# A first expert's weight chunks prefetched in every attention step, and its layer 1 begun one step later

## The chip, the cores and the metric

The kernel runs on one core of a Trainium2 chip. The metric is the device time of one execution in microseconds, the median of several runs.

## What is computed

Windowed attention with a few sink positions, then a mixture of experts on its output. A token goes to the best of four groups and to the best of four experts in it.

```python
B, H, S, D = 4, 8, 768, 64          # n_sink = 4, window = 128
keep = is_sink | in_window          # causal window of 128 positions
a = softmax(where(keep, q @ k.T / sqrt(D), -1e9))
x = (a @ v).transpose(0, 2, 1, 3).reshape(3072, 512)

g_logits = x @ w_group              # 512 x 4
e_logits = xg @ w_expert[g]         # 512 x 4 per group
h  = np.maximum(xg[mask_e] @ w1[g, e], 0.0)    # 512 x 1024
ye = h @ w2[g, e]                               # 1024 x 512
out[tok_idx] = combined[:, None] * ye           # both softmax weights
```

## The kernel before, in words

**Attention.** The 3072 tokens are 24 tiles of 128. The main loop runs over steps i = 0 to 25 and is a software pipeline: step i makes the scores of tile i, transposes the probabilities of tile i - 1 and copies them out of PSUM (`trans`, `evac`), multiplies tile i - 2 with its values in two blocks (`values(b, 0)` for the tile itself, `values(b, 1)` for the tile before and the sinks) and copies the result out (`out_evac`, the tile `xT`), and for tile i - 3 makes router logits and transposes back (`logits`, `natural`) and normalises and stores (`norm`, the tile `xt`). Steps 24 and 25 have no scores (they are not `live`). The values of tile 23 come in step 25, its logits behind the loop. All tiles share one PSUM bank `po` for the values and one pair of banks `tp` for the transposes.

**Routing.** Tokens are routed in four batches of six tiles. A generator emits the small VectorE operations of a batch in units; each step may take so many (`UNITS`, and 16 in steps 24 and 25). When the second batch has been counted, the largest expert so far is picked as first expert (`id0`); this happens in step 17. The first two gathers of its tokens are issued in steps 21 and 22, a third one ("late", from the third batch) behind attention.

**Weights.** A weight matrix of an expert comes in four chunks of 128x1024 floats (512 KB each): chunks 0 to 3 are the first expert's layer 1, 4 to 7 its layer 2, from 8 on comes the second expert. `prefetch` asks for chunks on SyncE's queue, into five raw buffers `rw` used in turn. `wjob` converts one: ScalarE copies it, rounded, to `whi`, and VectorE subtracts, `wlo = rw - whi`. In attention, step i's `wjob` casts the first half, the next step casts the second half, and the subtraction follows in the middle of the step behind that. From step 24 on a chunk is cast whole and subtracted at once.

**Layer 1 of the first expert** begins inside attention. `early_work` is a generator, `ew`: its first two turns transpose the two gathered token tiles, each further turn is one f of layer 1 (one of eight 128-column parts of the hidden layer, 12 matmuls of 128x256 over the four chunks; `ph` is its PSUM tile, `un` holds tokens and hidden values). Each engine executes its instructions in the order in which the program text emits them. An f is emitted at once, so a chunk that is not ready stops TensorE there. Behind attention `finish(ew)` runs the remaining f, then layer 2 of these tokens; on the way the late gather's tile is transposed (`xpose`). A small planner (`spend`) decides how many routing units and conversions are emitted behind each piece.

```python
if i > CHOOK and (i % 2 == 0 or i > NI - 4):
    prefetch(min(RAW, len(raws) + (1 if live else RAW)))
```

Of the kernel before, what the change touches and what calls it, by code (L numbers as in the profile page):

```python
# [24 lines left out]
NI = B * NT  # L25
# [3 lines left out]
NDC = DM // P  # L29
# [65 lines left out]
SNAP = 1  # L95
SNAPB = 2
DEPTH = 2
CHOOK = 15
PW = G + NE
WARM = 18  # L100
FILL = [8, 10, 6]
# [40 lines left out]
def moe_attention(tc, kqT, vN, vS, nsw, wgx, w1, w2, out):  # L142
    nc = Pinned(tc)
    v = nc.vector
    with ExitStack() as top, ExitStack() as att:
# [39 lines left out]
        def pair():  # L185
            return ps_p.tile([P, 2, 4 * P], F32, name="tp")

        def warm(k, dst=None):
            dst = pair()[:, 0, 0:192] if k and dst is None else dst
            for _ in range(k):  # L190
                nc.tensor.matmul(dst, wz[:, 0:P], wz, start=True, stop=True)
# [17 lines left out]
        def load_q(i):  # L209
            b, t = divmod(i, NT)  # L210
            nc.sync.dma_start(qb[:, i % NQ], kqT[b, t, :, KB:].rearrange("d (h q) -> d h q", h=HP))
# [138 lines left out]
        def put_gates(n):  # L350
            for _ in range(min(n, len(gates))):
                t, g = gates.pop(0)
                nc.sync.dma_start(xd[t * P:(t + 1) * P, DM:XW], g)
# [296 lines left out]
        def gather(r, j):  # L650
            w = min(P, CAPT[r] - j * P)
            cc = BASE[r] + j
            if (r, j) in TWIN:
                return
            for a, b in TWIN.items():
                if b[0:2] == (r, j):
                    wait_for(f"x{a[0]}")
                    w += 32
            xg[r, j] = t = gp.tile([P, XW], F32, name="xg")
            src = xd[0:sum(BATCHES[:(SNAP if j < EC else SNAPB) + 1]) * P] if r == 0 else xd  # L660
            nc.gpsimd.indirect_dma_start(
                out=t[0:w], out_offset=None, in_=src,
                in_offset=bass.IndirectOffsetOnAxis(ap=gidx[0:w, cc:cc + 1], axis=0))
# [6 lines left out]
        state = dict(issued=0, done=0, freed=0, credit=0.0, route=0.0, clk=0.0, at=0.0, dma=0.0, gap=PELAG, dve=0.0)  # L670

        def dve(us):
            state["dve"] = max(state["dve"], state["clk"]) + us
# [3 lines left out]
        def prefetch(depth):  # L677
            while len(raws) < depth and state["issued"] < len(chunks):
                k = state["issued"]
                if k - min([x[-1] for x in raws] + [x[-1] for x in held.values()], default=k) >= RAW + len(rawp) * RAWB:  # L680
                    return
                l, r, c = chunks[k]
                if (f"id{r}" if r < 2 else "eid") not in ready:
                    return
                state["issued"] += 1
                if r not in regs:
                    src = (eidi if r > 1 else eid01)[0:1, r:r + 1]
                    regs[r] = nc.nc.values_load(src, engines=[ENG.SP], min_val=0, max_val=NE - 1)
                e = bass.ds(regs[r], 1)
                rw = raw(k)[:, 0:F]  # L690
                if l == 1:
                    nc.sync.dma_start(rw, w1[e, c * P:(c + 1) * P, :].rearrange("o p f -> (o p) f"))
                else:
                    nc.sync.dma_start(rw.rearrange("p (k n) -> p k n", k=2),
                                      w2[e, 2 * c * P:(2 * c + 2) * P, :].rearrange("o (k p) n -> p (o k) n", p=P))
                state["dma"] = max(state["dma"], state["clk"] + DMALAG) + DMATIME
                if CAPT[r] <= 64:
                    held[l, r, c] = rw, k
                else:
                    raws.append((l, r, c, rw, state["dma"] + DMASLACK, k))  # L700

        def wjob(force=False):
            if tail:
                prefetch(RAW + RAWB)
            k = state["done"]
            if raws and not force and state["clk"] < raws[0][4]:
                return None
            if not raws or k >= state["freed"] + WBUF or (k % WBUF >= WA and len(wpool) < 2):
                return None
            l, r, c, rw, _, pos = raws.pop(0)  # L710
            wp = wpool[k % WBUF >= WA]
            hi = wp.tile([P, F], F32R, name="whi")
            lo = wp.tile([P, F], F32R, name="wlo")
            z = F if tail else F // 2
            nc.scalar.copy(hi[:, 0:z], rw[:, 0:z])

            def rest():
                v.tensor_tensor(lo, rw, hi.bitcast(F32), ALU.subtract)
                wt[l, r, c] = hi, lo
                if l == 2 and r in FEW:  # L720
                    held[l, r, c] = rw, pos
                if tail:
                    prefetch(RAW + RAWB)
            dve(1.2)
            state["done"] += 1
            if tail:
                rest()
                return True

            def more():  # L730
                nc.scalar.copy(hi[:, z:], rw[:, z:])
                return rest

            half.append(more)
            return None
# [442 lines left out]
        for i in range(NI + 2):  # L1178
            live = i < NI
            a, b, c = i - 1, i - 2, i - 3  # L1180
            mid, far, old = 0 <= a < NI, 0 <= b < NI, 0 <= c < NI
            state["clk"] += 3.0
            if i == NI:
                state.update(gap=0.0, dve=state["clk"])
                sps.close()
                put_gates(MAXB)
                while later:
                    gather(*later.pop(0))
                ps_h = fl.enter_context(tc.tile_pool(name="ps_h", bufs=4, space=PSUM, side="right", reuse_waits="tile"))
                tail.append(ps_h)  # L1190
                if rest:
                    rest()
                    rest = None
                if half:
                    half.pop()()()
            if live:
                scores(i, 0)
                scores(i, 1)
                if i + DEPTH < NI:
                    load_q(i + DEPTH)  # L1200
                warm(FILL[i] if i < len(FILL) else 0, ob[0][:, 224:416])
            if mid or old:
                env["tp"] = pair()
            if mid:
                trans(a)
                evac(a, 0)
                evac(a, 1)
            if far:
                values(b, 0)
                if b + 1 < NI:  # L1210
                    load_s(b + 1)
            if i + DEPTH < NI:
                load_k(i + DEPTH)
            if old:
                logits(c)
            if mid:
                sink_t(a)
            if old:
                natural(c)
            if live:  # L1220
                maxima(i, 0)
                exps(i, 0)
                maxima(i, 1)
            else:
                next(ew, None)
                if i == NI:
                    next(ew)
            if old:
                norm(c)
            routing(1, ("pe",))  # L1230
            if live:
                exps(i, 1, (0, 1))
            if mid:
                sink_evac(a)
            if live:
                exps(i, 1, (2, 3))
            if mid:
                sink_rows(a)
            if live:
                sink_pack(i)  # L1240
            if old:
                norm_logits(c)
            if i == 0:
                late_consts()
            state["clk"] += 3.0
            if far:
                values(b, 1)
                if live:
                    load_v(i)
                out_evac(b)  # L1250
            if rest:
                rest()
                rest = None
            put_gates(3 if live else MAXB)
            if live and later and not gates:
                gather(*later.pop(0))
            routing(UNITS.get(i, REND) if live else TSTEP, (None, "rd"))
            if live and i and i % 2 == 0:
                sums(i - 1)
            if i == NI:  # L1260
                sums(NI - 1)
            if live:
                rest = half.pop()() if half else wjob()
            if i > CHOOK and (i % 2 == 0 or i > NI - 4):
                prefetch(min(RAW, len(raws) + (1 if live else RAW)))
            if not live:
                wjob()
                next(ew, None)
        env["tp"] = pair()
# [308 lines left out]
```

## Time and profile before

| | before |
|---|---|
| median of 3 runs | 507.71 us (505.45 to 508.69) |
| profiled execution | 506.72 us, span 505.0 us |
| TensorE matmul, busy | 476.0 us, 94% of the span |
| VectorE / ScalarE / GpSimd busy | 376.5 / 329.6 / 168.9 us |
| TensorE's granted clock, mean | 0.979 |
| DMA traffic | 117.09 MB, mean 232 GB/s |

The span runs from the first to the last instruction. Granted clock is the share of full speed that TensorE's clock was given, 1.0 or 0.5 at a moment. Engines are PE (TensorE matmul), PEld (its weight load), DVE (VectorE), ACT (ScalarE), POOL (GpSimd), SPq (SyncE's DMA issues). In a timeline row the first number is the start in us, the second how long the instruction or the merged group took, then come engine, operation and out<-in tiles; a bracket gives the idle time of that engine just before, and what ended it. All kernel instructions go through one helper and so carry its line, 112.

### The profile page before, as it was taken

How to read it: one execution, taken by the hardware profiler on the slowest of the kernel's cores; microseconds unless marked ns; L12 is line 12 of the kernel's file. 1: busy time of each engine (PE TensorE's matmuls, PEld its weight loads, DVE VectorE, ACT ScalarE, POOL GpSimd, SP SyncE). 2: the span in 40 equal slices, each digit the busy share in tenths (PEclk: the TensorE clock that was granted, in tenths of full speed). 3: DMA queues.
4: the chain of work that ended last, by engine and by line, in shares of the span. 5: the costliest groups of instructions: out<-in, count | busy, mean ns of one | idle time of the engine just before them, and what ended most of it. 6: DMA issues, size and time to landing. Idle time of an engine off the chain costs nothing. (4 is left out here: it accounts for less than half of the span.)

```text
span 505.0 us, 14679 instructions
## 1 busy us (share of the span) xinstructions
PE 476.0 (94%) x5419; PEld 400.0 (79%) x5419; DVE 376.5 (75%) x1178; ACT 329.6 (65%) x856; POOL 168.9 (33%) x269
## 2 busy tenths in 40 slices
PE   7899999998975969999999999999999999999995
PEld 6688888877865958889798898759786878887974
DVE  7577898898866577997861775668767996999760
ACT  3999999888951234567742665557554786788651
POOL 3575765664680002403123120302330153102301
PEclk9999999999967999999999999999999999999998
DMA  8588888998893454684592446498669992999301
GB/s 237 166 270 271 286 265 252 266 300 231 279 312 105 159 198 142 201 295 163 203 411 86 121 145 228 123 353 324 201 245 334 387 380 88 326 369 380 122 0 49
DMA packets 59873, 117.09 MB, mean 232 GB/s; under 512 B 9758, under 2 KB 22046, under 8 KB 59792
## 3 DMA queue, kind: packets, MB, share of 16 engines
q1 hardware_dynamic: 54960, 102.50, 60.3%
q0 software_dynamic: 4304, 13.26, 8.1%
q8 instruction: 45, 0.74, 0.6%
q10 hardware_dynamic: 528, 0.29, 0.3%
q14 instruction: 36, 0.29, 0.2%
HBM read 103.25 MB, written 13.24 MB: 231 GB/s over the span
## 5 line engine op out<-in xcount | busy, mean ns | idle before, releaser
L112 DVE TENSOR_TENSOR wlo<-rw,whi 128x1024 fp32r<-128x1024 f32 x112 | 134.9, 1225 | 31.3 <-ACT whi L112 29.3
L112 PE MATMUL ph<-un,whi 128*128 128x256 f32 (+4 forms) x576 | 132.4, 318 | 1.2 <-ACT whi L112 1.0
L112 PE MATMUL po<-whi,un 128*128 128x512 f32 (+2 forms) x384 | 127.9, 396 | 0.0
L112 POOL DMA_INDIRECT out<-ot,sidx x33 | 42.8, 1298 | 239.0 <-ACT ot L112 96.3
L112 ACT CAST whi<-rw 128x1024 fp32r<-128x1024 f32 (+1 forms) x115 | 115.3, 1025 | 10.4 <-DMA rw<-in_w 6.7
L112 PE MATMUL ph<-un,wlo 128*128 128x160 f32 (+4 forms) x416 | 101.3, 268 | 4.4 <-DVE wlo L112 4.3
L112 PEld LDWEIGHTS ph<-un,whi 128*128 128x128 f32 x576 | 95.0, 191 | 3.2 <-ACT whi L112 1.2
L112 PEld LDWEIGHTS po<-whi,un 128*128 128x128 f32 (+1 forms) x384 | 70.8, 186 | 24.8 <-issue 6.7
L112 PEld LDWEIGHTS ph<-un,wlo 128*128 128x128 f32 x416 | 77.6, 190 | 5.7 <-DVE wlo L112 4.5
L112 ACT ACTIVATE pt<-sm,st 128x136 f32<-128x136 f32 x192 | 76.1, 402 | 6.6 <-DVE st L112 5.8
L112 PE MATMUL po<-wlo,un 128*128 128x512 f32 (+3 forms) x200 | 77.7, 390 | 2.2 <-DVE wlo L112 2.2
L112 DVE CUSTOM_DVE_ANT_0 sm<-ps,msk 128x136 f32<-128x136 f32 x192 | 45.8, 296 | 8.2 <-PE ps L112 1.7
L112 POOL DMA_INDIRECT xg<-xd,gidx x30 | 33.7, 1124 | 33.4 <-DMA rw<-in_w 21.0
L112 PEld LDWEIGHTS po<-wlo,un 128*128 128x128 f32 (+2 forms) x200 | 36.4, 182 | 10.1 <-DVE wlo L112 2.7
L112 PE MATMUL ps<-kb,qb 64*64 64x208 f32 (+1 forms) x768 | 39.2, 339 | 2.3 <-DMA qb<-in_kqT 1.8
L112 POOL COPY pu<-spT 32x512 f32<-32x512 f32 x48 | 29.8, 647 | 30.3 <-ACT spT L112 27.2
L112 ACT ACTIVATE un<-ph 128x256 fp32r<-128x256 f32 x40 | 15.3, 383 | 36.3 <-PE ph L112 35.5
L112 DVE TENSOR_TENSOR hc<-ph,hc 128x160 f32<-128x160 f32 (+2 forms) x64 | 21.8, 345 | 22.9 <-ACT hc L112 21.9
L112 ACT ACTIVATION_READ_ACCUMULATOR pt<-sm,st 128x1 f32 x192 | 36.8, 192 | 0.0
L112 ACT ACTIVATE ot<-po,cg 128x512 f32<-128x512 f32 (+3 forms) x25 | 17.0, 680 | 30.4 <-PE po L112 30.3
L112 PEld LDWEIGHTS ps<-kb,qb 64*64 64x64 f32 x768 | 27.1, 136 | 7.8 <-issue 3.4
L112 PE MATMUL po<-pa,vv 128*64 128x64 f32 x768 | 29.7, 233 | 3.4 <-POOL sp L112 1.8
(196 smaller groups left out, 726.1 us busy)
## 6 DMA issues: line engine op xcount, KB each, us to landing
rw<-in_w SPq DMA_DIRECT2D x128, 512.0 KB
vv<-in_vN SPq DMA_DIRECT2D x24, 512.0 KB
kb<-in_kqT SPq DMA_DIRECT2D x23, 288.0 KB
qb<-in_kqT SPq DMA_DIRECT2D x24, 256.0 KB
xd<-xt SPq DMA_DIRECT2D x24, 256.0 KB
vv<-in_vS SPq DMA_DIRECT2D x24, 128.0 KB
out<-ot,sidx POOLq DMA_INDIRECT x33, 8.3
xg<-xd,gidx POOLq DMA_INDIRECT x30, 5.4
```

The lines of the kernel that those rows point to most:

```text
L112: r = f(*a, **k)
```

## The change

Chunk prefetch starts at steps above 17 and is called in every step, not in every second one. At the start of step 24, conversions are forced until all four layer-1 chunks are done. At the ends of steps, `wjob` and a turn of `ew` come only behind step 24, so the first f of layer 1 moves from the end of step 24 to the middle of step 25 and the others follow one turn later.

```diff
-CHOOK = 15
+CHOOK = 17
...
                 if half:
                     half.pop()()()
+                while state["done"] < NDC:
+                    wjob(True)
             if live:
                 scores(i, 0)
...
-            if i > CHOOK and (i % 2 == 0 or i > NI - 4):
+            if i > CHOOK:
                 prefetch(min(RAW, len(raws) + (1 if live else RAW)))
-            if not live:
+            if i > NI:
                 wjob()
                 next(ew, None)
```

## Rows read from the trace of the kernel before

**Rows 1.** Windows by stage: PE, PEld, DVE, ACT, POOL busy us; clock, DMA share, GB/s.

```profile
130.00:140.00 10.00, 8.84 (x232) 7.48 (x224) 9.19 (x46) 9.48 (x34) 5.77 (x10) 1.00 0.97 310
...
150.00:160.00 10.00, 4.71 (x50) 3.90 (x48) 8.54 (x24) 2.96 (x5) 2.21 (x4) 0.84 0.42 139
```

**Rows 2.** Timeline of TensorE, from step 24 to the first expert's layer 2.

```profile
148.53 0.34 PE L112 MATMUL tp<-ident,sp 64*96 64x64 f32 x2 [0.55 <-POOL sp L112]
...
151.13 1.75 PE L112 MATMUL po<-pu,vv 96*64 96x64 f32 x32
...
159.94 0.58 PE L112 MATMUL ph<-un,wlo 128*128 128x256 f32 x1 [4.25 <-DVE wlo L112]
...
160.45 1.98 PE L112 MATMUL po<-pa,vv 128*64 128x64 f32 x32
...
166.45 1.15 PE L112 MATMUL po<-pu,vv 96*64 96x64 f32 x32
...
169.15 0.66 PE L112 MATMUL lg<-wsd,xT 128*64 128x40 f32 x16
...
169.74 0.47 PE L112 MATMUL tp<-ident,xT 64*128 64x64 f32 x8
...
173.69 0.46 PE L112 MATMUL ph<-un,whi 128*128 128x256 f32 x2
...
177.96 0.40 PE L112 MATMUL po<-whi,un 128*128 128x512 f32 x1
```

**Rows 3.** Timeline of VectorE and ScalarE in step 24.

```profile
151.00 0.69 DVE L112 TENSOR_TENSOR un<-ph,un 128x512 fp32r<-128x512 f32 x1 [3.26 <-ACT un L112]
...
153.59 0.59 ACT L112 COPY xT<-po 128x512 f32<-128x512 f32 x1
...
154.07 1.05 ACT L112 CAST whi<-rw 128x1024 fp32r<-128x1024 f32 x1
...
158.72 1.16 DVE L112 TENSOR_TENSOR wlo<-rw,whi 128x1024 fp32r<-128x1024 f32 x1
```

**Rows 4.** Timeline of ScalarE and VectorE at the start of step 24.

```profile
145.42 1.07 ACT L112 COPY pa<-tp 128x512 f32<-128x512 f32 x2
...
146.20 1.53 DVE L112 TENSOR_TENSOR wlo<-rw,whi 128x1024 fp32r<-128x1024 f32 x1
```

**Rows 5.** Timeline in step 21: a chunk's subtraction and GpSimd's select beside it.

```profile
128.70 1.22 DVE L112 TENSOR_TENSOR wlo<-rw,whi 128x1024 fp32r<-128x1024 f32 x1
128.77 1.66 POOL L112 TENSOR_SCALAR_AFFINE_SELECT pa<-pa 64x512 f32<-64x512 f32 x1
```

**Rows 6.** Timeline of GpSimd in step 24.

```profile
146.05 2.15 POOL L112 COPY pu<-spT 32x512 f32<-32x512 f32 x2
148.26 0.21 POOL L112 COPY sp<-pt 128x32 f32<-128x32 f32 x1
148.42 0.65 POOL L112 TENSOR_SCALAR_AFFINE_SELECT pu<-pa 64x512 f32<-64x512 f32 x1
```

**Rows 7.** Timeline of SyncE's DMA issues, steps 23 to 24.

```profile
143.91 4.23 SPq L112 DMA_DIRECT2D rw<-in_w  x4
```

**Rows 8.** Windows as in rows 1, finer, around the clock's changes.

```profile
152.00:153.00 1.00, 1.00 (x23) 0.93 (x20) 1.00 (x3) 0.00 (x0) 0.00 (x0) 0.75 0.78 250
...
158.00:160.00 2.00, 0.07 (x1) 0.07 (x1) 1.84 (x4) 0.00 (x0) 0.00 (x0) 0.83 0.18 16
...
166.00:167.00 1.00, 1.00 (x22) 0.87 (x22) 0.00 (x0) 0.38 (x1) 0.00 (x0) 0.93 0.16 57
```

**Rows 9.** Timeline behind attention: the late gather and two waits of TensorE.

```profile
175.75 0.97 POOL L112 DMA_INDIRECT xg<-xd,gidx  x1 [20.96 <-DMA rw<-in_w]
...
182.33 0.63 PE L112 MATMUL tp<-ident,xg 128*128 128x128 f32 x4 [1.61 <-DMA xg<-xd,gidx]
...
187.51 0.50 PE L112 MATMUL po<-wlo,un 128*128 128x512 f32 x1 [2.24 <-DVE wlo L112]
```

**Rows 10.** Waits of TensorE from 190 us: total, times, longest.

```profile
PE tp L112 <- DVE cg L112: 0.4, 1, 0.4
```

## Prediction

> **What bounds the kernel now.** I read the busy table by stage first, then TensorE's timeline where the table shows a hole, then what the other engines did at that moment, then the rest of the run. In attention all engines are near full and so is DMA, at 0.97 of its 16 engines [rows 1]. Between 150 and 160 us TensorE is busy for 4.71 of 10 us [rows 1]. Behind 190 us its longest kind of wait on a tile sums to 0.4 us [rows 10], so from there on TensorE sets the pace. What is won between 145 and 190 us therefore moves the end, if the weights and gathers move along.
>
> The hole is at the end of step 24 (the first step without scores). TensorE begins f=0 of the first expert's layer 1 and comes to weight chunk 3. It waits first for the high half and then 4.25 us for the low half [rows 2]. ACT cast the chunk at 154.07 us. DVE subtracts only at 158.72 us, because this subtraction stands behind the whole routing block of step 24 in DVE's program [rows 3]. Behind this wait, in TensorE's order, stands the rest of the last attention tile: its values start only at 160.45 us, its logits at 169.15 us [rows 2], though everything that the values need was ready some 6 us earlier (worked out below). A second price follows. The granted clock was 1.00 (2.4 GHz) before the wait. TensorE then idled for 4.25 us, the clock fell to half near 159.3 us (0.83 mean over 158 to 160) and rose again soon after 166 (0.93 over 166 to 167) [rows 8]. At half clock the 32 values matmuls took 1.98 us, at full clock 1.15 [rows 2].
>
> **The change, part by part.** I follow CHOOK, the prefetch condition, the forced conversion and the later layer 1.
>
> *Prefetch in every step.* Before, chunks 0 to 3 are asked for at the ends of steps 18, 20, 21 and 22, chunk 4 at the end of 23, chunks 5 to 7 at the start of 24. Afterwards steps 18 to 23 each ask for one (0 to 5), and the start of 24 asks for 6, 7 and 8. So on SP every old place carries the next chunk; step 19 gets a new load, and chunk 8 comes up from the end of step 24. CHOOK from 15 to 17 changes nothing: the expert's id is not known in step 16, and step 17 was odd. Conversion (half a chunk per step on ACT) keeps its slots: chunk 0 in 19 and 20, chunk 1 in 21 and 22, chunk 2 in 23 and 24. One more load of 512 KB enters the stretch before step 24. At the 310 GB/s of the nearest full stretch [rows 1] that is an estimated 1.7 us of DMA time. I cost it at nothing, since q, k and v are asked for up to two steps ahead; if that cover is gone, it costs 1.7 us. In step 24 SP waits for raw buffers: the four loads from 143.91 us take 4.23 us, the last held until chunk 2 is subtracted [rows 7]. Now the last is chunk 8 and waits for chunk 3's subtraction, about 1.2 us more. Behind it on SP stands the sink row load of tile 23, needed by the second values block one step later: covered.
>
> *Chunk 3 converted at the start of step 24.* On ACT its cast (1.05 us) lands between chunk 2's second half and the two copies of transposed probabilities that began at 145.42 and took 1.07 [rows 3, 4]. These end near 147.5 instead of 146.5. Their reader, POOL, begins on them only at 148.42 [rows 6]: covered. On DVE the subtraction follows chunk 2's, which ends at 146.20 + 1.53 = 147.73 [rows 4]. DVE then idles for 3.26 us until 151.00 [rows 3], so on DVE it is free. It is not free for POOL: a select beside a subtraction of 1.22 us took 1.66 us [rows 5], against 0.65 alone [rows 6]; so 1.0 us of delay. The two sink copies beside chunk 2's subtraction took 2.15 us [rows 6]. POOL's small pack copy at 148.26 is what TensorE waits for at 148.53 [rows 2, 6]. With a second subtraction right behind, I put that copy off by 1.2 us, a whole subtraction, since it would be asked for just behind its start; the bounds are 0 (POOL gets in between) and 1.5 (the longest subtraction here). This delays the rest of step 24.
>
> The Trainium skill speaks against this part of the change. "SBUF — State Buffer", section "Who interferes with whom", says that a DVE instruction with two SBUF inputs contends with a GpSimd instruction that reads SBUF, and that the loser is blocked for the whole instruction. By it the delay is a full subtraction. The trace agrees roughly: the select was held for 1.0 of 1.22 us [rows 5]. With 1.0 in place of 1.2 us the sum would grow by 0.2.
>
> *Layer 1 one step later.* f=0 goes to the middle of step 25, f=1 to its end, f=2 behind the loop, f=3 to 7 after attention. Taking it out of step 24 opens a wait that f=0 used to cover: the last tile's values write the bank that ACT copies out at 153.59 for 0.59 us [rows 3]. TensorE is free at 151.13 + 1.75 = 152.88 [rows 2] and starts the values at about 154.25: 1.3 us of new idling. This is the new latest wait.
>
> From there, with full-clock durations [rows 2]: values 1.15; logits 0.66 and natural transposes 0.47, less a little overlap, together 1.11; f=0, (177.96 - 173.69) / 3 = 1.42; second values block 1.15; f=1 1.42. The logits of tile 23 start at 154.25 + 6.25 = 160.5, against 169.15: 8.65 us earlier. DVE must have normalised tile 22 before the next transposes. Its routing block and sums end at 158.72 [rows 3], where the chunk no longer follows; with 0.7 us of normalising (a subtraction of the same 128x512 took 0.69 [rows 3]) it is ready at 159.4, in time. The POOL delay takes 1.2 off: 7.45.
>
> One f (1.42 us) is still owed by TensorE behind this point. It falls into two waits that exist already. The late gather is issued at 175.75, and TensorE waits 1.61 us for it; then 2.24 us for the low half of chunk 7, which DVE reaches only behind that tile's subtraction and nine routing operations [rows 9]. Both hang on the logits of tile 23 through DVE and POOL, not on TensorE. By the emission order the gather's transposes come one layer-2 step (0.7 us) earlier, and chunk 7 still stands behind the routing. I count 0.65 us as lost there: two more small DVE operations now stand between.
>
> **Sum.** 8.65 - 1.2 - 0.65 = 6.8 us. The profiled execution was 506.72 us (span 505.0), so it would take 499.9. It lies 1.0 below the median 507.71, and for that I forecast 500.9. A difference of 1%, 5.1 us, is about the least that I would tell from no change.
>
> **Rivals.** *Half clock.* Before, the clock rose in the second after 152 us [rows 8], behind unbroken work from 148.53. Afterwards that work starts later and is broken for 1.3 us. If the rise then comes only near 159.3, the values, logits, natural transposes and part of f=0, from 155.45 on, run at half clock: by the values rows [rows 2] 3.85 x (1 - 1.15 / 1.98) = 1.6 us more. Gain 5.2: 502.5. For it speaks that the clock fell and rose in just this stretch; against it, that it held for over six microseconds after the rise, four of them idle.
>
> *POOL is not held.* If the pack copy gets in ahead of the subtraction, the gain is 8.0: 499.7. The two copies' 2.15 us are compatible with either order.
>
> *The loads starve attention.* This ends slower. DMA stands at 0.97 in the last steps [rows 1]. Five chunks now lie one slot earlier; if in each of steps 19 to 23 the load delays k, q or v by its whole 1.7 us, 8.5 us are added and 509.4 results. It decides from the point where these delays sum to more than 6.8, four steps out of five. With only the one net load paid it gives 502.6. Against it: the slots on SP are the old ones, and TensorE's waits there are for ACT and POOL.
>
> *The change doesn't do it.* The forced conversion could find chunk 3 not landed. It is asked for in step 21, about two steps ahead, so I give this no chance of its own.
>
> **How the numbers follow.** Forecast 0.47 (500.9, own range 499 to 502.5), half clock 0.20, POOL not held 0.12, loads starve 0.15 (two thirds of it at the one-load price), something unseen in the emission order of routing and conversions 0.06. The range reaches from 497.5 (POOL not held and the new 1.3 us partly covered as well) to 506.0 (half clock and two loads paid). Under 502.6 lie the forecast, half of the half-clock case and POOL not held, 0.69; I lower that to 0.63, since half clock and loads can fall together. Slower by over 1% needs all steps starved and the half clock: 0.06. The rest, 0.31, is within 1%.
>
> **What would show it.** No wait for a low half of a weight chunk near 155 us; the last tile's values some 5 us earlier; chunk 3's subtraction directly behind chunk 2's; POOL's pack copy about a microsecond later than 148.26; a wait of near 1.3 us ahead of the last values; no second fall of the clock; the late gather some 7 us earlier, with waits for it and for chunk 7 still there. I am wrong if the scores of step 23 start more than 2 us later than before, or if the gather lands no earlier.

## The result, and the profile after

| | before | after |
|---|---|---|
| median of 7 runs, us | 505.88 (505.06 to 508.69) | 500.84 (499.11 to 503.45) |
| profiled execution, us | 506.72 | 500.27 |
| its span, us | 505.0 | 498.6 |

The runs of before are more than those shown ahead of the prediction, whence another median. The ratio of after to before is 0.990, with a 95% interval from 0.9868 to 0.9932: a gain of about 5 us, between 3.4 and 6.7. The forecast was 6.8, and 500.9 for the median. The two profiled executions lie 6.45 us apart. Ratios, here and below, leave disturbed executions out while medians take all, so that a ratio can differ by up to 0.4% from the quotient of the medians.

First the busy table by stage of the changed kernel, with the columns of [rows 1].

```profile
130.00:140.00 10.00, 8.86 (x236) 7.50 (x230) 9.19 (x46) 9.00 (x32) 6.40 (x12) 1.00 1.00 314
140.00:150.00 10.00, 7.60 (x122) 6.61 (x121) 7.71 (x20) 6.29 (x20) 9.66 (x11) 0.63 0.94 310
150.00:160.00 10.00, 8.82 (x106) 8.01 (x105) 8.14 (x24) 1.99 (x4) 1.81 (x3) 0.51 0.33 95
160.00:170.00 10.00, 10.00 (x124) 9.69 (x124) 6.14 (x18) 3.46 (x7) 0.82 (x1) 1.00 0.57 184
...
158.00:160.00 2.00, 2.00 (x13) 1.87 (x12) 1.04 (x4) 0.00 (x0) 0.00 (x0) 0.57 0.18 17
160.00:162.00 2.00, 2.00 (x41) 1.93 (x41) 0.00 (x0) 1.19 (x3) 0.00 (x0) 1.00 0.39 131
```

The hole is closed: TensorE is busy for 8.82 of the 10 us from 150 us on, against 4.71 [rows 1]. But the mean clock of that stretch is 0.51, so nearly all of it ran at 1.2 GHz, the lower level; it rose only shortly before 160 us. The clock had fallen well ahead of that: from 140 to 150 us its mean is 0.63, and in the kernel before it was 0.61, by this row of its busy table:

```profile
140.00:150.00 10.00, 7.61 (x120) 6.79 (x121) 6.75 (x19) 5.40 (x20) 9.44 (x14) 0.61 0.91 303
```

DMA from 130 to 140 us is at 1.00 against 0.97, and TensorE's busy time there is the same, 8.86 against 8.84.

TensorE's timeline of the changed kernel, to be read beside [rows 2] and [rows 9]; the bracket is the idle time before the group and what ended it.

```profile
135.44 1.64 PE L112 MATMUL ps<-kb,qb 64*64 64x208 f32 x32
...
148.12 0.34 PE L112 MATMUL tp<-ident,sp 64*96 64x64 f32 x2 [1.43 <-POOL sp L112]
...
150.72 1.98 PE L112 MATMUL po<-pu,vv 96*64 96x64 f32 x32
...
153.87 1.97 PE L112 MATMUL po<-pa,vv 128*64 128x64 f32 x32 [1.18 <-POOL pu L112]
...
162.62 0.67 PE L112 MATMUL lg<-wsd,xT 128*64 128x40 f32 x16
...
175.38 0.63 PE L112 MATMUL tp<-ident,xg 128*128 128x128 f32 x4 [0.53 <-DMA xg<-xd,gidx]
...
181.06 0.50 PE L112 MATMUL po<-wlo,un 128*128 128x512 f32 x1 [2.05 <-DVE wlo L112]
...
182.32 0.64 PE L112 MATMUL ph<-whi,un 128*128 128x512 f32 x2
```

No wait for chunk 3 is left. The last tile's values (`po<-pa`) start at 153.87 instead of 160.45 [rows 2], behind a new wait of 1.18 us. The bracket names GpSimd's copy into `pu`, but by the program these matmuls do not read it; they write the bank `po`, and ScalarE's copy out of that bank ends 0.10 us ahead of them:

```profile
153.18 0.59 ACT L112 COPY xT<-po 128x512 f32<-128x512 f32 x1
```

The logits of tile 23 start 6.53 us earlier (162.62 against 169.15), the late gather's transposes 6.95 earlier (175.38 against 182.33 [rows 9]). The wait for chunk 7 is still there, 2.05 us against 2.24 [rows 9]. The last line is the first matmul of tile 2's layer 1, which stood at 188.78 us before: 6.46 us earlier, and the whole difference of the profiles, since from it to the end of the span both need the same time (316.2 and 316.3 us). So everything is decided ahead of that line. TensorE's longest waits behind 185 us (total, times, longest) are as short as those of [rows 10]:

```profile
PE tp L112 <- DVE cg L112: 0.4, 1, 0.4
PE ph L112 <- DVE wlo L112: 0.3, 1, 0.3
```

The other engines at the start of step 24, to be read beside [rows 4], [rows 6] and [rows 7], and the issue of the late gather [rows 9]:

```profile
142.83 5.54 SPq L112 DMA_DIRECT2D rw<-in_w  x4
...
144.76 2.15 POOL L112 COPY pu<-spT 32x512 f32<-32x512 f32 x2
...
144.91 3.08 DVE L112 TENSOR_TENSOR wlo<-rw,whi 128x1024 fp32r<-128x1024 f32 x2
...
146.97 1.09 POOL L112 COPY sp<-pt 128x32 f32<-128x32 f32 x1
...
169.18 0.97 POOL L112 DMA_INDIRECT xg<-xd,gidx  x1 [14.80 <-DMA rw<-in_w]
```

Two subtractions now stand together on VectorE, chunk 2's and chunk 3's, 3.08 us. GpSimd's pack copy, 0.21 us before [rows 6], takes 1.09 beside the second one, and TensorE's wait for it is 1.43 us, where it was 0.55 [rows 2]. SyncE's four loads, the last of them chunk 8, take 5.54 us instead of 4.23 [rows 7], 1.3 more, and nothing that the trace shows waits for it.

### The profile page after: what moved, and what is told of

Its sections match the earlier page's. It is cut to its first block, busy times and chain, and to the rows that moved or that the text cites. A ratio compares the mean times of both kernels' runs of the same rounds, so it can differ in the third digit from the quotient of the medians.

```text
span 498.6 us, 14682 instructions
## 1 busy us (share of the span) xinstructions
PE 475.2 (95%) x5419; PEld 399.5 (80%) x5419; DVE 376.9 (76%) x1178; ACT 330.1 (66%) x856; POOL 167.0 (33%) x269
## 5 line engine op out<-in xcount | busy, mean ns | idle before, releaser
L112 POOL DMA_INDIRECT out<-ot,sidx x33 | 41.3, 1252 | 241.6 <-ACT ot L112 97.2
L112 POOL DMA_INDIRECT xg<-xd,gidx x30 | 32.5, 1083 | 27.2 <-DMA rw<-in_w 14.8
```

The lines of the kernel that those rows point to most:

```text
L112: r = f(*a, **k)
```

## The experiments

The theory: the gain comes from TensorE no longer waiting for chunk 3 behind the routing block; part of it is lost to the half clock and to GpSimd's held copy. Rivals: the earlier loads do it, or later layer 1 alone does it, or the parts work against each other. Each ratio is to the kernel before on the same chip; the median of before there is 506.68 us for the first four, 507.77 for the next four and 506.49 for the last four.

| kernel | median, us | ratio to before | 95% interval | TensorE waits for a low half of the first expert's chunks, us |
|---|---|---|---|---|
| the change | 500.84 | 0.990 | 0.9868 to 0.9932 | 2.05 (chunk 7) |
| e1, force only | 495.62 | 0.9778 | 0.9734 to 0.9821 | none |
| e2, later only | 500.95 | 0.9884 | 0.9828 to 0.9941 | 2.17 and 2.02 |
| e3, prefetch only | 506.44 | 0.9998 | 0.9967 to 1.0029 | 4.26 (chunk 3) |
| e4, subtract late | 499.03 | 0.9819 | 0.9774 to 0.9864 | 2.03 (chunk 7) |
| e5, conversion kept | 501.23 | 0.9827 | 0.9775 to 0.988 | none |
| e6, layer 1 kept | 501.2 | 0.989 | 0.9853 to 0.9926 | 1.09 (chunk 7) |
| e7, force and prefetch | 498.42 | 0.9832 | 0.9793 to 0.987 | none |
| e8, gaps filled | 500.0 | 0.9852 | 0.9818 to 0.9887 | 2.06 (chunk 7) |
| e9, the change again | 501.12 | 0.9922 | 0.9888 to 0.9957 | 2.05 (chunk 7) |
| e10, force and fill | 494.35 | 0.9781 | 0.974 to 0.9821 | none |
| e11, force, subtract late | 497.46 | 0.9848 | 0.981 to 0.9886 | none |
| e12, change with chunk 7 | 496.94 | 0.9828 | 0.9791 to 0.9865 | none |

**e1: the forced conversion alone**, in the kernel before.

```diff
                     half.pop()()()
+                while state["done"] < NDC:
+                    wjob(True)
```

> Only the forced conversion at the start of step 24 is added to the kernel before; prefetch and the place of layer 1 stay. Theory (the wait for chunk 3's low half behind the routing block is what is won): the 4.25 us wait goes, f=0 also fills TensorE's gap ahead of the last values, gain 5 to 7 us. Rival order (the gain comes from taking f=0 out of the last tile's way): f=0 still stands there, gain under 2 us.

Measured: 495.62 us, ratio 0.9778. One of the change's edits gives 11 us, twice the whole change and well above the 5 to 7 us expected. Its profile, TensorE's timeline:

```profile
148.92 0.26 PE L112 MATMUL tp<-ident,sp 64*96 64x64 f32 x2 [2.24 <-POOL sp L112]
...
154.57 1.15 PE L112 MATMUL po<-pa,vv 128*64 128x64 f32 x32
...
160.77 0.67 PE L112 MATMUL lg<-wsd,xT 128*64 128x40 f32 x16
...
174.27 0.91 PE L112 MATMUL tp<-ident,xg 128*128 128x128 f32 x4 [1.98 <-DMA xg<-xd,gidx]
...
179.79 0.63 PE L112 MATMUL ph<-whi,un 128*128 128x512 f32 x2
```

The last values have no wait in front (f=0, still in step 24, fills it) and run at the full clock, 1.15 us. There is no wait for chunk 7 between the gather's transposes and tile 2's layer 1. VectorE's timeline of weight subtractions tells why; first e1's, then the changed kernel's:

```profile
145.72 3.08 DVE L112 TENSOR_TENSOR wlo<-rw,whi 128x1024 fp32r<-128x1024 f32 x2
...
158.21 1.16 DVE L112 TENSOR_TENSOR wlo<-rw,whi 128x1024 fp32r<-128x1024 f32 x1
...
160.91 1.23 DVE L112 TENSOR_TENSOR wlo<-rw,whi 128x1024 fp32r<-128x1024 f32 x1 [0.62 <-ACT whi L112]
...
169.83 1.23 DVE L112 TENSOR_TENSOR wlo<-rw,whi 128x1024 fp32r<-128x1024 f32 x1 [1.05 <-issue]
...
171.31 1.22 DVE L112 TENSOR_TENSOR wlo<-rw,whi 128x1024 fp32r<-128x1024 f32 x1
```

```profile
162.76 1.23 DVE L112 TENSOR_TENSOR wlo<-rw,whi 128x1024 fp32r<-128x1024 f32 x1 [3.59 <-ACT whi L112]
...
172.94 1.23 DVE L112 TENSOR_TENSOR wlo<-rw,whi 128x1024 fp32r<-128x1024 f32 x1 [1.67 <-ACT whi L112]
...
174.42 1.22 DVE L112 TENSOR_TENSOR wlo<-rw,whi 128x1024 fp32r<-128x1024 f32 x1
...
179.78 1.23 DVE L112 TENSOR_TENSOR wlo<-rw,whi 128x1024 fp32r<-128x1024 f32 x1
```

Count them: behind the pair, e1 subtracts chunk 4 at 158.21 (the conversion at the end of step 24), 5, 6, and 7 at 171.31, all ahead of the last batch's routing. The changed kernel has no conversion at the end of step 24, so 4, 5 and 6 take the places ahead of the routing and 7 comes at 179.78, behind it. In the kernel before, chunk 7 stood behind the routing too: there the conversion at the end of step 24 went to chunk 3. The expectation had counted neither this wait nor the full clock behind chunk 3; how the 11 us divide among them is not shown by any run.

**e2: layer 1 and the conversion later, alone.**

```diff
-            if not live:
+            if i > NI:
                 wjob()
```

> Only the later layer 1 is taken from the change: no forced conversion, old prefetch. Chunk 3 is then converted when f=0 asks for it in the middle of step 25, on VectorE still behind the routing block of step 24. Theory: TensorE does the last values' first block, logits and transposes during that time, then waits about 2 us for the low half near 158 to 160 us; gain 2.5 to 5 us, less than the force alone. Rival order: the whole gain of the change, 5 us or more, as the force is not needed.

Measured: 500.95, ratio 0.9884, as much as the change, and a little above the 2.5 to 5 us expected. In its timeline of TensorE chunk 3 is still late, but the wait is half of what it was [rows 2], since the last values are done ahead of it:

```profile
152.74 1.15 PE L112 MATMUL po<-pa,vv 128*64 128x64 f32 x32 [1.27 <-POOL pu L112]
...
158.40 0.58 PE L112 MATMUL ph<-un,wlo 128*128 128x256 f32 x1 [2.17 <-DVE wlo L112]
...
181.88 0.76 PE L112 MATMUL po<-wlo,un 128*128 128x512 f32 x1 [2.02 <-DVE wlo L112]
```

So the forced conversion and the later layer 1 are two cures for one wait, and their gains do not add.

**e3: the prefetch alone.**

```diff
-CHOOK = 15
+CHOOK = 17
...
-            if i > CHOOK and (i % 2 == 0 or i > NI - 4):
+            if i > CHOOK:
```

> Only the prefetch in every step from step 18 is taken from the change. Theory: chunk 3 was never late by its load, so no gain, within 1 us of the kernel before, and the 4.25 us wait is still there. Rival loads (weights that come earlier make the gain): 3 us or more. If the loads starve attention: up to 1.7 us slower for the net load, with later scores of step 23.

Measured: 506.44 in 12 runs, ratio 0.9998. The earlier loads cost nothing and bring nothing by themselves: TensorE waits 4.26 us for chunk 3, as before, in its timeline:

```profile
160.83 0.58 PE L112 MATMUL ph<-un,wlo 128*128 128x256 f32 x1 [4.26 <-DVE wlo L112]
```

**e4: chunk 3's subtraction late**: in the changed kernel its cast stays at the start of step 24, its subtraction moves to just ahead of the routing block.

```diff
                 while state["done"] < NDC:
-                    wjob(True)
+                    subs.append(wjob(True, True))
...
+            while subs:
+                subs.pop()()
             routing(UNITS.get(i, REND) if live else TSTEP, (None, "rd"))
```

> The whole change, but of chunk 3's conversion only the cast stays at the start of step 24; the subtraction is put just ahead of the routing block of step 24. Theory (GpSimd is held by the second subtraction): GpSimd's pack copy is short again (0.2 us) and TensorE's wait for it falls from 1.43 us to about 0.5; 1 us more is won than by the change, gain 6 to 7 us; up to 1.5 us more if the clock then rises before step 25. Rival (GpSimd is not what matters there): the same time as the change, gain 5 us.

Measured: 499.03, ratio 0.9819; the interval's upper end, 0.9864, lies just under the change's lower end, 0.9868, on another chip. Its timeline of GpSimd's and TensorE's two instructions:

```profile
149.91 0.21 POOL L112 COPY sp<-pt 128x32 f32<-128x32 f32 x1
...
150.18 0.26 PE L112 MATMUL tp<-ident,sp 64*96 64x64 f32 x2 [1.36 <-POOL sp L112]
...
155.81 1.15 PE L112 MATMUL po<-pa,vv 128*64 128x64 f32 x32 [1.50 <-POOL pu L112]
```

The copy is back at 0.21 us, so the subtraction is what stretches it. TensorE's wait is 1.36 us all the same. The last values ran at the full clock here (1.15 us, against 1.97 in the change), so what e4 gained can as well be the clock's. e11 asks again about the copy.

**e5: the conversion at the end of step 24 kept**, in the changed kernel, layer 1 still later; and **e6: layer 1 kept** in step 24, the conversion gone. Together they split the last edit.

```diff
-            if i > NI:
+            if not live:
                 wjob()
+            if i > NI:
                 next(ew, None)
```

> The whole change, but the ordinary conversion at the end of step 24 stays (chunk 4 there, chunk 5 in step 25); layer 1 still begins one step later. Theory A (dropping that conversion is what the change gives away against the force alone: one conversion less before the routing, so chunk 7 stands behind it and TensorE waits 2 us): that wait is gone, 2 to 3 us more than the change, gain 7 to 8 us against the kernel before. Theory B (the later f=0 gives it away: the gap ahead of the last values stays empty and one f more is owed): gain as the change, 5 to 6 us.

```diff
             if i > NI:
                 wjob()
+            if not live:
                 next(ew, None)
```

> The whole change, but layer 1 begins where it did (f=0 at the end of step 24); the conversion at the end of step 24 stays dropped. Theory A: the wait of 2 us for chunk 7 is still there, gain 5.5 to 7 us. Theory B: f=0 fills the 1.2 us gap and one f (1.4 us) less is owed, so nearly the force alone, gain 8 to 11 us.

Measured: e5 0.9827, with no wait for chunk 7 in its trace; e6 0.989, the change's own ratio, with the wait at 1.09 us behind a longer one for the gather, in TensorE's timeline:

```profile
175.68 1.03 PE L112 MATMUL tp<-ident,xg 128*128 128x128 f32 x4 [2.02 <-DMA xg<-xd,gidx]
...
181.30 0.50 PE L112 MATMUL po<-wlo,un 128*128 128x512 f32 x1 [1.09 <-DVE wlo L112]
```

The traces put the wait for chunk 7 on the dropped conversion, and where f=0 stands makes no difference that can be seen once chunk 3 is ready. By time alone e5 doesn't settle it: its interval overlaps those of e6 and of the change, and the execution that was profiled (504.12 us) is one of its two slowest. e12 asks this again.

**e7: the last hunk undone**, force and prefetch kept.

```diff
-            if i > NI:
+            if not live:
                 wjob()
                 next(ew, None)
```

> Force and prefetch in every step, with layer 1 and the conversion at the end of step 24 left as before: the change without its last edit. Both theories: as the force alone, gain 10 to 11 us, since the prefetch alone gave nothing. Rival (prefetch hurts beside the force): under 9 us.

Measured: 498.42, ratio 0.9832, a gain of 8.5 us, under the 10 to 11 expected and on the side of the rival. But the interval overlaps that of e1 (0.9778); whether the prefetch takes something away beside the forced conversion isn't told apart.

**e8: the two gaps filled** with 9 and 7 idle matmuls in the changed kernel, so that TensorE has no pause there.

```diff
+            if i == NI + 1:
+                warm(7, spare()[:, 0:192])
...
+            if i == NI:
+                warm(9, spare()[:, 0:192])
```

> The whole change, with 9 idle matmuls (128x192, results unused) ahead of the pack transposes of step 24 and 7 ahead of the last values, where TensorE waited 1.43 and 1.18 us. If the half clock behind these gaps sets the end: the clock is full again before step 25, 1.5 to 3 us more than the change, gain 6.5 to 8 us. If the late gather and VectorE set it: no more than 0.5 us beyond the change, and longer waits at the gather instead.

Measured: 500.0, ratio 0.9852. Its row of the busy table shows the clock held; busy time counts the idle matmuls:

```profile
150.00:160.00 10.00, 8.46 (x159) 7.69 (x156) 8.06 (x24) 3.10 (x7) 3.20 (x6) 1.00 0.45 143
```

The interval, 0.9818 to 0.9887, overlaps the change's. By the ratios the full clock would be worth some 2.4 us (0.990 - 0.9852 = 0.0048 of 506), by the intervals anything from nothing up.

**e9: the change again**, unaltered, on the chip of e10 to e12.

> The changed kernel itself, unaltered, on the same chip as the three runs beside it, since kernels before were compared over different chips. Both theories: ratio 0.988 to 0.992 to the kernel before, as when it was first timed.

Measured: 501.12 in 12 runs, ratio 0.9922. Its row of the busy table for the stretch in question:

```profile
150.00:160.00 10.00, 7.78 (x120) 7.23 (x114) 7.39 (x24) 2.56 (x5) 2.26 (x4) 0.83 0.53 161
```

The same program, and a clock of 0.83 here against 0.51 in the profile above. From the scores of step 23 to tile 2's layer 1 it takes 44.1 us in this execution, by these rows of TensorE's timeline, and 46.9 in the other (135.44 to 182.32):

```profile
135.61 1.64 PE L112 MATMUL ps<-kb,qb 64*64 64x208 f32 x32
...
179.73 0.63 PE L112 MATMUL ph<-whi,un 128*128 128x512 f32 x2
```

This profiled run, 496.62 us, is the fastest of its twelve.

**e10: force alone, with 9 idle matmuls** ahead of the pack's transposes.

```diff
                 while state["done"] < NDC:
                     wjob(True)
...
+            if i == NI:
+                warm(9, spare()[:, 0:192])
```

> The force alone, with 9 idle matmuls (128x192, results unused) where TensorE waits for GpSimd's pack copy in step 24. If a half clock behind that wait costs time: 1 to 3 us beyond the force alone, gain 11 to 13 us. If the late gather sets the pace there: as the force alone, 9 to 11 us.

Measured: 494.35, ratio 0.9781, that of e1. From 150 to 160 us the mean clock is 1.00 in its profile and 0.83 in e1's, so the filling held the clock; a gain from that does not show in the ratio.

**e11: force alone, with the subtraction behind the two token tiles' own subtractions**, so that GpSimd's copy isn't beside it.

```diff
+                while state["done"] < NDC:
+                    subs.append(wjob(True, True))
...
                     next(ew)
+                while subs:
+                    subs.pop()()
```

> The force alone, but chunk 3's subtraction behind the two token tiles' subtractions of step 24 instead of ahead of them, so that GpSimd's pack copy is not held (0.2 instead of 1.1 us) while f=0 still gets its low half in step 24. Theory (GpSimd's hold is a cost of the force): TensorE's wait for the pack copy is 0.9 us shorter, 0 to 1 us beyond the force alone, part of it given back since tile 21 is normalised 1.2 us later. If the hold costs nothing: no better than the force alone.

Measured: 497.46, ratio 0.9848, no better than e1. In its timeline, the copy is short again, TensorE's wait for it is 1.35 us (2.24 in e1), and the last values have a wait that e1 doesn't have:

```profile
148.24 0.21 POOL L112 COPY sp<-pt 128x32 f32<-128x32 f32 x1
...
148.51 0.34 PE L112 MATMUL tp<-ident,sp 64*96 64x64 f32 x2 [1.35 <-POOL sp L112]
...
155.39 1.15 PE L112 MATMUL po<-pa,vv 128*64 128x64 f32 x32 [1.17 <-POOL pu L112]
```

In these two traces, what freeing GpSimd gives is mostly lost at the next wait: counted from the scores of step 23, the pack's transposes come 1.46 us earlier than in e1, the last values only 0.23. The price of the held copy on the end is not shown by any run.

**e12: the change, and chunk 7 forced** right behind the first expert's layer 1, ahead of the routing.

```diff
                     finish(ew)
+                    while state["done"] < 2 * NDC:
+                        wjob(True)
```

> The whole change, with chunk 7 converted right behind the first expert's layer 1 (forced), ahead of the late gather's tile and the routing units in VectorE's order. Theory A (what the change gives away against the force alone is mostly this chunk's wait): TensorE's wait of 2 us for chunk 7 goes, 1.5 to 2.5 us beyond the change on the same chip. Rival (the wait only moves to the next late thing, the routing or the second tile): under 0.7 us beyond it.

Measured: 496.94, ratio 0.9828 against 0.9922 for the change on the same chip; the intervals don't meet. TensorE's and VectorE's timelines:

```profile
174.24 0.63 PE L112 MATMUL tp<-ident,xg 128*128 128x128 f32 x4 [0.70 <-DMA xg<-xd,gidx]
...
175.08 1.22 DVE L112 TENSOR_TENSOR wlo<-rw,whi 128x1024 fp32r<-128x1024 f32 x1
...
176.21 0.69 DVE L112 TENSOR_TENSOR un<-tp,un 128x512 fp32r<-128x512 f32 x1
...
179.38 0.63 PE L112 MATMUL ph<-whi,un 128*128 128x512 f32 x2
```

Chunk 7 is subtracted at 175.08, ahead of the token tile's subtraction (the next line) and so of the routing, and no wait for a low half is left. That the last chunk behind the routing costs the change part of its gain is shown. The medians differ by 4.2 us, the wait was 2.05; where the other 2 us come from isn't: the two profiled stretches are 43.0 and 44.1 us, but the second is of the change's fastest run.

## Why the prediction was right, and where it was off

**The hole.** Right, and shown: TensorE's wait for chunk 3 is what the change removes. e3 leaves it (4.26 us) and gains nothing; e1 and e2 each attack it and gain.

**The new latest wait.** Right: 1.18 us ahead of the last values, forecast 1.3. e6, where f=0 stays in step 24, doesn't have it and is no faster.

**GpSimd's hold.** The mechanism is shown, the size a little under: the copy grew by 0.88 us (1.09 - 0.21); 1.2 was forecast. e4 and e11 take the second subtraction away, and the copy is 0.21 us again. I had put the copy just behind the subtraction's start; it began at 146.97, when the subtraction had run for half a microsecond (from 146.4), and ended at 148.06, just behind it (147.99). By the Trainium skill ("SBUF — State Buffer", section "SBUF: two separate sides") the engine that comes second is blocked until the other's instruction is done; the trace agrees: the copy was held for 0.88 us, up to the subtraction's end. What the hold costs on the path is not shown. TensorE's wait for the copy is 0.88 longer than before too (1.43 - 0.55), but with the short copy it was 1.36 us in e4, 1.35 in e11, and in e3, which has no second subtraction there at all, this:

```profile
149.17 0.21 POOL L112 COPY sp<-pt 128x32 f32<-128x32 f32 x1
...
149.43 0.34 PE L112 MATMUL tp<-ident,sp 64*96 64x64 f32 x2 [1.35 <-POOL sp L112]
```

These are e3's timelines of GpSimd and TensorE. The wait varies with when TensorE arrives, and the agreement of 0.88 with 0.88 proves nothing.

**The logits of tile 23.** Here a rival came in. Forecast 8.65 - 1.2 = 7.45 us earlier, measured 6.53. The parts, by TensorE's rows: the pack's transposes began 0.41 earlier than before (148.12 against 148.53), not 1.2 later. With 0.88 of hold, step 24 itself was 1.29 earlier, as the sink copies show (144.76 against 146.05 [rows 6]). I forecast nothing there and no run explains it: from step 23's scores to GpSimd's pack copy e3, whose edits I had costed at nothing, took 0.7 us less than before (12.3 against 13.0), and e9, the same program as the change, 0.7 less than the change (10.8 against 11.5), so single executions differ by as much. The values of the first block took 1.98 instead of 1.75 us, but that was absorbed: the wait behind them was 0.19 shorter than the 1.37 between 152.88 and 154.25, since ScalarE's copy of the bank came 0.41 earlier (153.18 against 153.59 [rows 3]), just as the pack's transposes did. So the last values began at 153.87, and not at 154.25 + 1.2. From them to the logits I counted 6.25 us at the full clock; it took 162.62 - 153.87 = 8.75. That is the half clock: 2.5 us, where the rival had 1.6, because all of the work up to shortly before 160 us ran at it, not only from 155.45 on. The rival's mechanism was right: the clock, which before had risen in the second after 152 us [rows 8], now rose only behind the pause, shortly before 160 us. The kernel before had paid the same: there this stretch took 169.15 - 160.45 = 8.70 us [rows 2], behind its long wait. My sum counted on winning that back, and in this execution none of it was won: the last values are 6.58 us earlier, the logits 6.53. In e8 the clock is held, and in e9's profile mostly; there the stretch to tile 2's layer 1 is 44.5 and 44.1 us against 46.9.

**The late gather and chunk 7.** Right that both waits stay (0.53 and 2.05 us). The 0.65 us that I counted as lost there was about 0.1 (6.53 earlier at the logits, 6.46 at tile 2's layer 1). What I did not do is ask why chunk 7 stays behind the routing. I wrote that it does, and took it as given; it is the change's own last edit that keeps it there, by dropping the conversion at the end of step 24.

**The loads.** Right: costed at nothing. The scores of step 23 start at 135.44 us, and before at 135.25, by this row of TensorE's timeline:

```profile
135.25 1.64 PE L112 MATMUL ps<-kb,qb 64*64 64x208 f32 x32
```

e3's ratio is 0.9998. The rival of starved attention falls, and so the slower side.

**The sum.** 6.8 us forecast; 6.45 between the profiles, about 5 between the medians. That the median of 500.84 meets the forecast of 500.9 is luck: the gain was 1.8 us smaller than forecast, and the median of before 1.8 us lower. In the profiled execution the half clock (-2.5) was nearly paid back by step 24's start (+1.29), the smaller hold (+0.32) and the smaller loss at the gather (+0.6). The term that was mis-sized is the clock's: the sum put the last tile at the full clock throughout. The mean clock of every execution is on record: 0.976 to 0.989 in the change's seven (0.979 in the profiled one), 0.978 to 0.992 in e9's twelve, 0.982 to 0.998 in e8's six. So the clock of the first profile is nearer to the common case than that of e9's, which is the highest of its twelve. The rest, from 6.45 to about 5, is not explained by the half clock of that profile, which the 6.45 already holds; the profiled execution of before lay 0.84 above its median and that of the change 0.57 below, and what spreads the executions is not shown.

**What the change leaves.** The two cures for chunk 3 don't add (e2 equals the change), and the last edit moves one conversion past the routing (e12). Force alone (0.9778) beats both kernels, and with the filling (0.9781) it is the same; these are the best versions that ran, and the second was on one chip with the change (0.9922), where the intervals don't meet. The change keeps about half of what its best part gives.

## What to carry to other kernels

In an engine's in-order program, ask of every conversion on which side of the long block it stands, for the chunk that you look at and for the last one of the queue: a conversion dropped early comes due later, for another chunk. Where two edits remove the same wait, run each alone, since their gains don't add and one may carry a cost of its own. Where the clock is at its lower level in the stretch that a change closes up, cost the work there at both levels, from the point where it will start, and put the difference into the range.

## What the runs showed of the hardware

The granted clock differs between executions of one program: 0.51 and 0.83 over the same 10 us, with 46.9 and 44.1 us for the stretch around them. The Trainium skill ("TensorE: Matmul & The Clock Gate", section "What's actually happening") says that the number of matmuls at the lower level, as a kernel starts, varies from run to run of the same kernel. These traces show the like in the middle of one. The 2.8 us between them, half a per cent of the run, are more than half of what this change gained.

VectorE's two-input subtractions and GpSimd's copies slowed each other here. The two subtractions took 3.08 us in a row beside the sink copies and the pack copy, where two alone would take 2.4 (1.22 and 1.23 us each elsewhere); the sink copies took 2.15 us, against 1.16 at 153.22 us of the same trace, and the pack copy five times its own time.
